# Cosformer attention into a two-layer FFN on one core: the third batch's x by DMA transposes, the first batch's result stored later, the order made anew

## The chip, the cores and the metric

The kernel runs on one core of a Trainium2 chip. The time is what the device takes for one execution, in microseconds (us); several runs are taken and their median is given. The engines are named as in the profile: PE is the matrix engine (TensorE), PEld its weight loads, DVE the VectorE, ACT the ScalarE, POOL the GpSimd, and SP the engine whose queue issues nearly all DMAs.

## The reference

Eight batches of attention with eight heads, 576 tokens and 64 features per head, with a linear (cosine) kernel, and then an FFN over all 4608 tokens:

```
phi(x) = concat(relu(x) * cos(theta), relu(x) * sin(theta))        # 64 -> 128 features
kv  = einsum('bhsf,bhsd->bhfd', phi(k), v);  z = sum over s of phi(k)
x   = (phi(q) @ kv) / (phi(q) . z + 1e-6)                          # 4608 x 512
h   = x @ w_in;  g = max(0.01 * h, h);  out = g @ w_out            # 512 -> 2048 -> 512
```

All inputs and the output are float32. The kernel rounds to float16 for the matmuls.

## The kernel before

Of each batch the first 512 tokens are the main part: 128 partitions by j = 0 to 3. The last 64 tokens of all eight batches together make a ninth group, number 8. So the FFN runs over nine groups g of 512 tokens. Batches are counted from 0 in the code and in this text: "batch 2" is the third.

For one batch the work is a chain. load_main and load_kvtail bring q, k and v (1 MB each, k and v with two tails of 64 KB) over the SP queue into a pool of three staging tiles. q_part and k_part apply phi on DVE or ACT (as the table ON says), v_part rounds v into the one tile vmain and its tails into vtail. kv_all forms kv and z on PE and copies them out on ACT. q_transpose_dma turns phi(q) of one j by a DMA transpose (qp to qpT). num multiplies it with kv on PE and divides on DVE (the small addition before it, den, on DVE or ACT), which gives xs, one j of x. x must then be turned (xT: features on partitions). For batches 3 and later x_transpose_dma does it with a DMA transpose on the SP queue; for batch 2 x_transpose does it with four PE transposes for each j into PSUM and one ACT copy out. Batches 0 and 1 have code of their own ahead of all this.

From group 2 on both layers of the FFN are computed with seven products of half-size blocks in place of eight, in Strassen's manner. In the first layer x_sums makes the sums of x's blocks on DVE, p1 is one product (four matmuls of 256 columns) into one of four PSUM banks, and seed, lrelu, u_copy, u_add and u_lrelu move it out. Product 1 (n = 1) needs only the xT of j = 0 and 1; the sums need all four. In the second layer g_sums makes the sums of g, p2 is four matmuls of one product, two banks a and b hold the results, and o_copy (ACT) and o_add (DVE) bring them into output tiles "ob" of two j each. Product 6 is added onto product 1 in bank a, after o_copy has read product 1 from there. o_store sends half of a group's 512 rows (512 KB). Group 1's first layer (f1_pair) is plain and runs while batch 2 goes through its attention; its second layer is in the seven products. Group 0's second layer is plain too: ffn2_out copies each of its four results into a tile "osb" and stores it at once, 256 KB each.

The order from batch 2 on is a table, PLACE: each step is put on a list with a number, the list is sorted by it, and the engines' instructions are issued in that order. What counts is the order on each engine: every engine and the SP queue works through its own instructions one after the other, and one that waits holds up those behind it. A DMA on SP also waits until the one eight before it has landed. A pool's tile is taken again only when its last readers are done, DMAs among them.

The first layer's and the second's matmuls are all on PE, and the two layers of neighbouring groups are interleaved in it, so that one fills the waits of the other.

Of the kernel before, what the change touches and what calls it, by code (L numbers as in the profile page):

```python
# [9 lines left out]
dt = mybir.dt  # L10
# [3 lines left out]
P = 128  # L14
# [4 lines left out]
def kernel(  # L19
# [14 lines left out]
    nc = tc.nc  # L34
# [35 lines left out]

    early = pool("early", 4, stack=first)
    pairpool = pool("pair", 2, stack=first)
    gpool = pool("g", 1, stack=first)
    opool = pool("osb", 4, stack=first)
# [410 lines left out]
    def x_transpose(g, j):  # L485
        xs = st["xs", g, j]
        ps = psum("o", [P, NKC, P], dt.float16, "ps_xt")
        for c in range(NKC):
            nc.tensor.transpose(ps[:, c, :], xs[:, 2 * c : 2 * c + 2, :], ident)
        nc.scalar.copy(xT_tile(g, j), ps)  # L490

# [63 lines left out]
    def ffn2_out(g, tt, eng):  # L555
        osb = opool.tile([P, DM], dt.float32, name="osb", tag="osb")
        copy(eng, osb, st["ps_o", g, tt])
        nc.sync.dma_start(out_rows(g)[:, tt, :], osb)
# [219 lines left out]
    opool = pool("out", 3)  # L778
# [287 lines left out]
    def open_seed():  # L1066
# [11 lines left out]
            16, 101, 252, 406, 552, 699, 827, 945,  # L1078
        ),
        "f1_pair": (  # L1080
            56, 57, 23, 24, 17, 18, 39, 42, 27, 28, 34, 35, 50, 51, 63, 70,
        ),
        "open_banks": (
            76,
        ),
        "open_seed": (
            77,
        ),
# [13 lines left out]
        ),  # L1102
        "seed": (
            100, 122, 168, 240, 259, 283, 309, 384, 408, 457, 483, 529, 569, 581, 612, 672, 712,
            734, 773, 822, 836, 868, 893, 935, 947, 988, 1003,
        ),
        "lrelu": (
# [4 lines left out]
        ),  # L1112
        "u_copy": (
# [4 lines left out]
        ),  # L1118
        "u_add": (
# [4 lines left out]
        ),  # L1124
        "u_lrelu": (
            186, 219, 248, 302, 326, 390, 402, 439, 486, 528, 543, 574, 610, 663, 697, 746, 775,
            805, 834, 869, 894, 932, 959, 977, 1018, 1038, 1041,
        ),
        "f1_one": (
            102, 104, 139, 147, 154, 155, 222, 224,  # L1130
        ),
        "o_tiles": (
            96, 228, 399, 546, 709, 854, 963, 1058,
        ),
# [204 lines left out]
```

## Time and profile before

| | us |
|---|---|
| median of three runs | 272.4 |
| lowest and highest | 272.4, 273.26 |
| the profiled execution's own time | 273.75 |
| its span, from the first to the last instruction | 271.9 |

Mean clock of PE in the profiled execution: 0.998. Busy shares of the span: PE 97%, PEld 82%, DVE 77%, ACT 72%, POOL 3%; the transfers of the SP queue fill 83.3% of 16 DMA engines' span. 57.05 MB were moved.

Rows of a timeline give the start and the length in us, then engine, line, operation and tiles. A row of groups gives a line, engine, operation, tiles and shapes, the count, busy us and mean ns of one, and the idle time of the engine just before them with what ended it. A row of stretches gives the stretch and its length, then busy us and count for PE, PEld, DVE, ACT and POOL, the granted clock of PE, the DMA share and GB/s. A matmul's busy time includes the way through the array, so neighbouring ones overlap.

### The profile page before, as it was taken

What the parts mean: (1) busy time and instruction counts of PE and PEld (TensorE: products, weight loads), DVE (VectorE), ACT (ScalarE), POOL (GpSimd) and SP (SyncE); (2) the same over time, 40 slices, a digit from 0 to 9 for tenths busy, and PEclk for the clock granted to TensorE, in tenths of its full rate; (3) what the DMA queues carried; (4) which work ended last, traced back from release to release, by engine and by line L of the source; (5) the groups of instructions that cost most, each with busy time, mean ns of one, the idle gap of its engine ahead of it and who ended that gap; (6) DMA issues with size and microseconds to landing.
All of it is one profiled execution on the core that took longest, in us unless ns stands there. A gap on an engine that the chain in (4) does not pass through costs nothing.

```text
span 271.9 us, 6680 instructions
## 1 busy us (share of the span) xinstructions
PE 263.6 (97%) x2703; PEld 221.8 (82%) x2703; DVE 209.3 (77%) x439; ACT 196.9 (72%) x329; POOL 8.1 (3%) x20
## 2 busy tenths in 40 slices
PE   8899999999999999999999999999999999999994
PEld 3585465555788989999999999999999889999983
DVE  4884998997969988999789869995686666765741
ACT  7675544786977887898687987887888766775621
POOL 2131011000000000000000000000000000000000
PEclk9999999999999999999999999999999999999999
DMA  6999999999999999999999999497178321300126
GB/s 216 382 384 403 381 410 356 292 221 239 222 306 226 238 199 226 301 174 246 224 266 209 244 284 269 80 194 176 39 82 195 112 55 68 157 0 2 77 80 154
DMA packets 82942, 57.05 MB, mean 210 GB/s; under 512 B 54496, under 2 KB 76000, under 8 KB 82400
## 3 DMA queue, kind: packets, MB, share of 16 engines
q1 hardware_dynamic: 82608, 56.37, 83.3%
q8 instruction: 21, 0.34, 0.6%
q10 hardware_dynamic: 304, 0.26, 0.4%
q14 instruction: 9, 0.07, 0.1%
HBM read 36.70 MB, written 9.44 MB: 170 GB/s over the span
## 4 chain that ended last, share of the span: by engine, by line
PE 72%; DMA 18%; ACT 3%; SPq 3%; DVE 1%; issue 1%; POOL 0%; ACTq 0%
PE ps_o L972 31%; PE ps_h L879 30%; DMA w2st<-in_moe_w_out_dram 6%; DMA w1st<-in_moe_w_in_dram 4%; PE ps_h L972 3%; DMA kpr<-in_k_dram 3%; DMA vst<-in_v_dram 3%; PE ps_num L417 2%; DMA qst<-in_q_dram 2%; SPq L130 2%; PE ps_kv L316 2%; ACT g L852 2%; PE ps_h L830 2%; PE ps_o L542 1%; ACT kp L254 1%
## 5 line engine op out<-in xcount | busy, mean ns | idle before, releaser
L972 PEld LDWEIGHTS <-g 128*128 128x128 f16 x640 | 62.2, 98 | 6.7
L267 DVE TENSOR_TENSOR u<-ps_h,u 128x512 f32<-128x512 f32 x54 | 37.1, 687 | 19.7 <-PE ps_h L879 17.9
L879 PEld LDWEIGHTS <-w 128*128 128x128 f16 x432 | 46.8, 114 | 1.4 <-issue 0.2
L972 PE MATMUL ps_o<-w,g 128*128 128x256 f16 x352 | 46.9, 273 | 0.0
L899 ACT COPY u<-ps_h 128x512 f32<-128x512 f32 x54 | 31.6, 586 | 9.8 <-PE ps_h L879 9.5
L892 ACT ACTIVATE g<-ps_h 128x512 f16<-128x512 f32 x54 | 31.9, 599 | 7.2 <-PE ps_h L879 6.4
L879 PEld LDWEIGHTS <-wa 128*128 128x128 f16 x324 | 33.5, 106 | 2.4
L879 PE MATMUL ps_h<-xw,w 128*128 128x256 f16 x216 | 32.1, 273 | 0.0
L879 PE MATMUL ps_h<-xT,w 128*128 128x256 f16 x216 | 31.8, 273 | 0.0
L972 PE MATMUL ps_o<-wb,g 128*128 128x256 f16 x232 | 31.5, 273 | 0.0
L879 PE MATMUL ps_h<-xw,wa 128*128 128x256 f16 x216 | 31.4, 273 | 0.0
L906 ACT ACTIVATE g<-u 128x1024 f16<-128x1024 f32 x27 | 28.7, 1062 | 2.9 <-DVE u L267 2.8
L990 ACT COPY ob<-ps_o 128x512 f32<-128x512 f32 (+1 forms) x32 | 18.0, 562 | 14.0 <-PE ps_o L972 11.9
L972 PEld LDWEIGHTS <-gs 128*128 128x128 f16 x256 | 24.6, 98 | 2.4
L435 DVE TENSOR_TENSOR xs<-ps_num,rden 128x512 f16<-128x512 f32 x28 | 19.3, 691 | 1.3
L830 PE MATMUL ps_h<-xT,w 128*128 128x512 f16 x80 | 19.2, 379 | 1.0 <-ACT g L852 1.0
L889 ACT COPY ps_h<-ps_h 128x512 f32<-128x512 f32 x27 | 15.7, 581 | 3.9 <-PE ps_h L879 3.5
L267 DVE TENSOR_TENSOR ob<-ps_o,ob 128x512 f32<-128x512 f32 (+1 forms) x22 | 14.8, 674 | 3.0 <-PE ps_o L972 2.0
L972 PE MATMUL ps_o<-wb,gs 128*128 128x256 f16 x120 | 17.0, 273 | 0.0
L972 PE MATMUL ps_o<-w,gs 128*128 128x256 f16 x120 | 16.5, 273 | 0.0
L879 PE MATMUL ps_h<-xT,wa 128*128 128x256 f16 x108 | 16.2, 273 | 0.0
L542 PE MATMUL ps_o<-w,g 128*128 128x512 f16 x64 | 15.6, 379 | 0.2 <-DVE w L264 0.2
(116 smaller groups left out, 392.1 us busy)
## 6 DMA issues: line engine op xcount, KB each, us to landing
qst<-in_q_dram SPq DMA_DIRECT2D x7, 1024.0 KB, 8.1
out_dram<-ob SPq DMA_DIRECT2D x14, 512.0 KB, 3.6
kst<-in_k_dram SPq DMA_DIRECT2D x6, 1024.0 KB, 7.2
vst<-in_v_dram SPq DMA_DIRECT2D x6, 1024.0 KB, 7.7
w1st<-in_moe_w_in_dram SPq DMA_DIRECT2D x8, 512.0 KB, 11.1
w2st<-in_moe_w_out_dram SPq DMA_DIRECT2D x4, 1024.0 KB, 13.1
vpr<-in_v_dram SPq DMA_DIRECT2D x4, 576.0 KB, 11.0
kpr<-in_k_dram SPq DMA_DIRECT2D x3, 576.0 KB, 11.1
```

What stands on the lines that cost most here:

```text
L130: nc.sync.dma_start(st[nm, b][:, lo:hi].rearrange("p c j d -> p c (j d)"), flat[:, lo:hi])
L267: nc.vector.tensor_tensor(out=o, in0=a, in1=b, op=ALU.add)
L435: nc.vector.tensor_tensor(out=xs, in0=ps[:, :, 0 : 4 * NE].rearrange("p a (b e) -> p a b e", e=NE)[:, :, :, 0:D], in1=rden.rearrange("p (a ...
L542: nc.tensor.matmul(ps, lhsT=st["g", g][:, m, tt * P : (tt + 1) * P], rhs=w2[:, m, :], start=(m == 0), stop=(m == NFT - 1),)
L830: nc.tensor.matmul(ps, lhsT=w1[m // 4][c // 2][:, c % 2, m % 4 : 512 : 4], rhs=st["xT", g][:, c], start=(c == 0), stop=(c == NKC - 1),)
L879: nc.tensor.matmul(bank[:, p], lhsT=w(c), rhs=x_blocks(g)[n][:, c], start=(fresh and p == 0 and c == 0), stop=(c == 1), skip_group_check=True,
L889: nc.scalar.copy(bank1[bj], bank1[bi])
L892: nc.scalar.activation(st["g" + nm, g][:, 2 * t : 2 * t + 2], bank1[bi], AF.Lrelu)
L899: nc.scalar.copy(st["u", g, t][:, n], bank1[bi])
L906: nc.scalar.activation(st["gt", g][:, :, 1, 2 * t : 2 * t + 2], st["u", g, t], AF.Lrelu)
L972: nc.tensor.matmul(bank, lhsT=st[G2[n], g][:, m, pair * P : (pair + 1) * P], rhs=W2[n](m), start=(fresh and m == 0), stop=(m == NH - 1), s ...
L990: nc.scalar.copy(o_at(g, half_, col, pair), bank_of(bi, pair, pair is None))
```

## The change

Three things are done. Batch 2's x is turned by DMA transposes like that of the later batches; x_transpose is gone. The output tiles' pool "out" (three) is split: two of its tiles ("out") are there from the start, one ("out1") opens later as before. Group 0's results go into the two early ones instead of four "osb" tiles, and are stored as two halves of 512 KB by o_store, at places of the table. And the table PLACE, with ON, is another one throughout.

```
-    opool = pool("osb", 4, stack=first)
+    outpool = pool("out", 2)
...
-    def x_transpose(g, j):
-        xs = st["xs", g, j]
-        ps = psum("o", [P, NKC, P], dt.float16, "ps_xt")
-        for c in range(NKC):
-            nc.tensor.transpose(ps[:, c, :], xs[:, 2 * c : 2 * c + 2, :], ident)
-        nc.scalar.copy(xT_tile(g, j), ps)
...
     def ffn2_out(g, tt, eng):
-        osb = opool.tile([P, DM], dt.float32, name="osb", tag="osb")
-        copy(eng, osb, st["ps_o", g, tt])
-        nc.sync.dma_start(out_rows(g)[:, tt, :], osb)
+        half_, pair = divmod(tt, 2)
+        if ("ob", g, half_) not in st:
+            st["ob", g, half_] = outpool.tile([P, 2, DM], dt.float32, name="ob", tag="ob")
+        copy(eng, st["ob", g, half_][:, pair], st["ps_o", g, tt])
...
-    opool = pool("out", 3)
+    opool = pool("out1", 1)
...
     def o_tiles(g):
-        for half_ in range(2):
-            st["ob", g, half_] = opool.tile([P, 2, DM], dt.float32, name="ob", tag="ob")
+        st["ob", g, 0], st["ob", g, 1] = (
+            pool_.tile([P, 2, DM], dt.float32, name="ob", tag="ob") for pool_ in (outpool, opool)
+        )
...
         "o_store": (
-            264, 347, 437, 500, 575, 615, 747, 956, 819, 872, 996, 1014, 1073, 1078,
+            225, 333, 390, 512, 568, 930, 763, 689, 870, 830, 986, 958, 1067, 1080, 192, 76,
         ),
...
+    for half_ in range(2):
+        put(o_store, 0, half_)
...
-            put((x_transpose_dma, x_transpose)[b == 2], b, j)
+            put(x_transpose_dma, b, j)
```

On the SP queue, from batch 2's v load (the first row) on, before. qpT<-qp are transposes of phi(q), first of batch 2, then of batch 3; qst, kst, vst and the tails ktl, vtl are the loads, from the third row on of batch 3.

```order
L103 DMA vst<-in_v_dram 128x8x256
L113 DMA vtl<-in_v_dram 64x4x64 x2
L558 DMA out_dram<-osb 128x512 x4
L385 DMA_TRANSPOSE qpT<-qp 128x8x128 x2
L103 DMA qst<-in_q_dram 128x8x256
L385 DMA_TRANSPOSE qpT<-qp 128x8x128 x2
L103 DMA kst<-in_k_dram 128x8x256
L113 DMA ktl<-in_k_dram 64x4x64 x2
L385 DMA_TRANSPOSE qpT<-qp 128x8x128
L103 DMA vst<-in_v_dram 128x8x256
L113 DMA vtl<-in_v_dram 64x4x64 x2
```

And the same stretch of the SP queue in the changed kernel, up to batch 4's q. xT<-xs are the transposes of batch 2's x, in the order j = 3, 0, 1, 2; out_dram<-ob is the second half of group 0's result.

```order
L104 DMA vst<-in_v_dram 128x8x256
L114 DMA vtl<-in_v_dram 64x4x64 x2
L386 DMA_TRANSPOSE qpT<-qp 128x8x128 x2
L104 DMA qst<-in_q_dram 128x8x256
L386 DMA_TRANSPOSE qpT<-qp 128x8x128
L104 DMA kst<-in_k_dram 128x8x256
L114 DMA ktl<-in_k_dram 64x4x64 x2
L386 DMA_TRANSPOSE qpT<-qp 128x8x128
L104 DMA vst<-in_v_dram 128x8x256
L114 DMA vtl<-in_v_dram 64x4x64 x2
L397 DMA_TRANSPOSE xT<-xs 128x4x128
L992 DMA out_dram<-ob 128x1024
```

The four stores of group 0 have left the place ahead of the transposes, one transpose fewer stands between the loads of q and v, and the transposes of x and a store stand behind v.

On ACT, before, from the copies of batch 2's turned x to the first cast of batch 3's v (vmain<-vst): ob<-ps_o is o_copy of group 1's first product, ps_h<-ps_h a seed, g and u the moving out of group 2's first products, qp and kp phi of batch 3.

```order
L490 COPY xT<-ps_xt 128x4x128
L254 ACTIVATE qp<-qst,cos_t 128x8x64
L254 ACTIVATE kp<-kst,cos_t 128x8x64 x2
L990 COPY ob<-ps_o_1235 128x2x256
L254 ACTIVATE kp<-kst,sin_t 128x8x64
L889 COPY ps_h_1233<-ps_h_1231 128x512
L254 ACTIVATE kp<-kst,cos_t 128x8x64
L863 ACTIVATE g<-ps_h_1232 128x2x256
L899 COPY u<-ps_h_1231 128x512
L262 CAST vmain<-vst 128x16x64
```

And on ACT in the changed kernel, from the last first-layer activations of group 1 (g<-ps_h) to the seed; den is a divide of batch 2.

```order
L846 ACTIVATE g<-ps_h 128x2x2x256
L255 ACTIVATE kp<-kst,cos_t 128x8x64
L846 ACTIVATE g<-ps_h 128x2x2x256
L431 ACTIVATE den<-ps_num,eps 128x8
L255 ACTIVATE kp<-kst,sin_t 128x8x64
L846 ACTIVATE g<-ps_h 128x2x2x256
L263 CAST vmain<-vst 128x16x64 x2
L985 COPY ob<-ps_o_1183 128x2x256
L255 ACTIVATE kp<-kst,sin_t 128x8x64
L883 COPY ps_h_1181<-ps_h_1179 128x512
```

The casts of v's main part, one on ACT before and two now, have moved from behind the first o_copy and the seed to ahead of both. The tile that this o_copy writes is the one from which the second half of group 0 is stored.

More of the change, by code (lines that the diff above doesn't have):

```diff
@@ L1077 @@
         "quarters": (
-            16, 101, 252, 406, 552, 699, 827, 945,
+            13, 112, 245, 400, 536, 699, 834, 951,
         ),
         "f1_pair": (
-            56, 57, 23, 24, 17, 18, 39, 42, 27, 28, 34, 35, 50, 51, 63, 70,
+            31, 32, 14, 18, 48, 54, 58, 60, 25, 26, 37, 39, 22, 23, 64, 67,
         ),
         "open_banks": (
-            76,
+            68,
         ),
         "open_seed": (
-            77,
+            72,
         ),
         "p1": (
[12 rows of a table removed]
[12 rows of a table added]
         ),
         "seed": (
-            100, 122, 168, 240, 259, 283, 309, 384, 408, 457, 483, 529, 569, 581, 612, 672, 712,
@@ L1128 @@
+            789, 829, 877, 913, 941, 962, 989, 1008, 1034, 1053,
         ),
         "f1_one": (
-            102, 104, 139, 147, 154, 155, 222, 224,
+            114, 116, 147, 150, 159, 160, 201, 202,
         ),
         "o_tiles": (
-            96, 228, 399, 546, 709, 854, 963, 1058,
+            84, 243, 405, 564, 718, 858, 970, 1060,
         ),
         "p2": (
[14 rows of a table removed]
[14 rows of a table added]
         ),
         "o_copy": (
-            97, 136, 174, 203, 229, 294, 330, 374, 400, 440, 480, 515, 547, 605, 638, 659, 710,
@@ L1153 @@
-            743, 770, 800, 855, 889, 906, 940, 964, 1009, 1025, 1045, 1064, 1071, 1086, 1097, 1059,
-            1085, 1095, 1100,
+            85, 115, 158, 203, 244, 275, 321, 359, 406, 458, 486, 532, 565, 598, 621, 658, 719,
+            745, 774, 803, 859, 881, 904, 932, 971, 1000, 1024, 1057, 1072, 1081, 1088, 1106, 1061,
+            1079, 1085, 1097,
         ),
         "o_add": (
-            146, 188, 213, 271, 348, 396, 428, 492, 558, 588, 642, 675, 740, 777, 804, 858, 918,
-            943, 976, 1032, 1068, 1091, 1087, 1110, 1082, 1101, 1107,
+            130, 194, 219, 282, 330, 380, 407, 493, 531, 582, 650, 674, 731, 793, 827, 862, 911,
@@ L1159 @@
+            957, 1006, 1035, 1062, 1091, 1098, 1112, 1092, 1094, 1108,
         ),
         "o_store": (
-            264, 347, 437, 500, 575, 615, 747, 956, 819, 872, 996, 1014, 1073, 1078,
+            225, 333, 390, 512, 568, 930, 763, 689, 870, 830, 986, 958, 1067, 1080, 192, 76,
         ),
         "o_store_tail": (
-            1092, 1104, 1108, 1111, 1109,
+            1093, 1100, 1107, 1113, 1110,
         ),
         "w1_sums": (
-            52, 178, 10, 13, 14, 325,
+            62, 109, 271, 294, 306, 299,
@@ L1203 @@
         ),
         "num": (
-            65, 49, 60, 53, 161, 190, 141, 131, 292, 280, 304, 337, 446, 429, 481, 461, 622, 576,
-            600, 590, 735, 772, 782, 757, 864, 888, 849, 873,
-        ),
-        "x_transpose": (
-            73, 61, 66, 62,
+            50, 70, 63, 55, 156, 182, 146, 172, 310, 326, 295, 342, 433, 467, 449, 489, 581, 630,
+            597, 606, 749, 725, 758, 776, 878, 890, 854, 836,
+        ),
+        "x_transpose_dma": (
+            82, 93, 94, 75, 163, 185, 177, 195, 318, 327, 354, 378, 478, 468, 511, 490, 620, 634,
+            639, 673, 775, 773, 797, 810, 910, 912, 897, 895,
@@ L1221 @@
         ),
         "load_qtail": (
-            676, 665, 702, 684,
+            777, 728, 769, 707,
         ),
@@ L1227 @@
         "k_part": (
-            "VVVAAAAVAVVVAAAVAVVVVVVVVVVAVVVAAAAVAVVAVAAVVVAVVVVAVVVVAAVA"
+            "VVVVVVAVAVVAAVVAAVVVVAAVAVVVVVAVVAAVVVAVVAAVAVVAVVAVVVAVVVVA"
         ),
         "q_part": (
-            "AVVAVVVAAVVVAVVAAAAAAVVVVAAAVVVAAVVVVVAVVVVAAAVAAAVAAAVA"
+            "AAAAAAVVVVAAVAVAAVVVVAVAAAVAVAAVVVVAVAVVVVVAAVVVAAVVVVVV"
         ),
         "v_part": (
-            "VVAAVVVAVVVVAVVAVV"
+            "VVAAAVAVVVVAVVVAAA"
         ),
         "num": (
-            "VVVVVVAVAVAVVVVVVVVVVVAVVVAV"
+            "AVAVVAAAAVVVVVVVAVVVVVVAVAVA"
         ),
```

28 lines of the change are left out of this document (12 added, 16 removed), and 102 rows, old and new, of the table PLACE.

## The prediction

> **What bounds the kernel now.** I read the page first.
>
> ```profile
> span 271.9 us, 6680 instructions
> PE 263.6 (97%) x2703; PEld 221.8 (82%) x2703; DVE 209.3 (77%) x439; ACT 196.9 (72%) x329; POOL 8.1 (3%) x20
> DMA  6999999999999999999999999497178321300126
> ```
>
> TensorE (PE) is busy for 97% of the span, and the DMA engines are full for the first two thirds. To see where the two meet I cut the span into stretches around the place that the change touches: before batch 2's x is used, the twelve microseconds after, and the rest.
>
> ```profile
> 50.90:73.28 22.38, 21.31 (x183) 13.56 (x182) 20.61 (x47) 18.02 (x27) 0.00 (x0) 1.00 1.10 230
> 73.28:82.00 8.72, 8.20 (x99) 7.21 (x97) 6.22 (x17) 6.85 (x12) 0.00 (x0) 1.00 1.14 310
> 82.00:262.00 180.00, 180.00 (x1890) 166.83 (x1889) 139.80 (x286) 139.89 (x237) 0.00 (x0) 1.00 0.78 166
> ```
>
> The first two columns are the length and PE's busy time; the last two are the DMA share and GB/s. From 82 us to 262 us PE never waits, so nothing there can be gained but work taken off PE. In the first stretch it waits 22.38 - 21.31 = 1.07 us, in the second 8.72 - 8.20 = 0.52 us, and there the DMA share is above 1: the transfers are saturated. The chain of waits for that region, and the issues on the SP queue (timeline), say which transfers:
>
> ```profile
> 57.86 6.57 DMA qst<-in_q_dram
> 65.87 1.82 ACT g L852 x2
> 67.69 1.54 ACT xT L490 x3
> 69.63 7.39 DMA vst<-in_v_dram
> 77.05 0.69 DVE vmain L264
> ...
> 50.72 3.18 SPq L558 DMA_DIRECT2D out_dram<-osb  x4
> 54.08 3.68 SPq L385 DMA_TRANSPOSE qpT<-qp  x2
> 59.52 4.76 SPq L385 DMA_TRANSPOSE qpT<-qp  x2
> 64.33 0.57 SPq L103 DMA_DIRECT2D kst<-in_k_dram  x1
> 66.46 3.12 SPq L385 DMA_TRANSPOSE qpT<-qp  x1
> ```
>
> Batch 3's q lands at 57.86 + 6.57 = 64.43, its v at 69.63 + 7.39 = 77.02. Between these two landings, in 12.6 us, the queue served two transposes of q, k with its tails, one more transpose and v. So around 50 to 80 us the end is set by what the DMA queue can deliver, and after 82 us by PE alone.
>
> **The change, part by part.** (1) TensorE loses 16 transposes, ScalarE (ACT) four copies out of PSUM.
>
> ```profile
> L489 PE MATMUL ps_xt<-ident,xs 128*128 128x128 f16 x16 | 1.4, 219 | 0.1
> L490 ACT COPY xT<-ps_xt 128x512 f16<-128x512 f16 x4 | 2.2, 589 | 0.0
> 48.44 0.45 PE ps_xth L474 x8
> ```
>
> The 219 ns are each one's own time; in a row they start 0.45 / 8 = 56 ns apart (eight like ones of batch 0), so PE is relieved of 16 x 56 ns = 0.9 us. The Trainium skill, "TensorE: Matmul & The Clock Gate", Part 4 on the PE-mode transpose, gives about 275 ns for one in a kernel; priced so, the change would save 4.4 us instead, and my time would come out 3.5 us lower. The trace's spacing decides against that price. The four copies, 2.2 us, stood in the chain at 67.69; they go with the waits below.
>
> (2) The four 256 KB stores of the first batch leave the SP queue at 50.72, and two of 512 KB take their place later: the first stands right behind batch 3's v load, the second some 20 us further on, where I see no reader waiting behind it. SP gets to the transposes of q 54.08 - 50.72 = 3.4 us sooner. The stores were 1.05 MB, at 295 GB/s (the mean of 40 to 60 us, next row) 3.5 us of transfer. So I take q to land 3.4 us sooner, at 61.0; had part of the stores' time been idle time of the queue, 2 us sooner, at 62.4.
>
> ```profile
> 40.00:60.00 20.00, 19.37 (x192) 11.27 (x190) 18.73 (x39) 13.82 (x22) 1.00 (x1) 1.00 1.06 295
> 57.85:59.80 1.95, 1.95 (x25) 1.22 (x23) 1.95 (x5) 1.74 (x3) 0.00 (x0) 1.00 1.10 217
> 71.12:77.03 5.91, 5.91 (x53) 5.24 (x51) 4.94 (x12) 5.02 (x9) 0.00 (x0) 1.00 1.21 235
> ```
>
> (3) The order of the SP queue. Between the landings of q and v there now stands one transpose less (256 KB, at the 217 GB/s of its stretch 1.2 us; I take 1.0): v lands at 61.0 + 12.6 - 1.0 = 72.6. Bounds: 71.3 if the loads of 1.2 MB each run at the 260 GB/s and better that single stretches show, 74.0 with the late q. Behind v now stand, in this order, its tails (128 KB), a transpose of x (128 KB), the store of half of batch 0's result (512 KB) and two more transposes of x (256 KB). At 250 GB/s, between the rows above, the store lands 3.1 us after v, at 75.7, and the x tiles of tokens 0 to 255 1.0 us after it, at 76.7; bounds for the store 2.6 us (the 310 GB/s of the second stretch) and 3.5 us (217).
>
> (4) The order on ACT. Before, the copy of batch 1's first output tile (o_copy) came ahead of any cast of batch 3's v. Now both casts of v's main part stand ahead of it, and it writes into the tile from which batch 0's half is stored, so it waits for that store also.
>
> ```profile
> L262 ACT CAST vmain<-vst 128x1024 f16<-128x1024 f32 x4 | 4.2, 1049 | 0.7 <-DMA vst<-in_v_dram 0.7
> L990 ACT COPY ob<-ps_o 128x512 f32<-128x512 f32 x28 | 16.5, 589 | 8.9 <-PE ps_o L972 8.8
> L972 PE MATMUL ps_o<-w,g 128*128 128x256 f16 x352 | 46.9, 273 | 0.0
> 94.16 2.62 PE ps_o L972 x24
> ```
>
> ACT sits at the first cast until v lands: 72.6 + 2 x 1.05 = 74.7; the store holds it to 75.7; o_copy ends at 75.7 + 0.59 = 76.3. Queued behind it on ACT are a seed copy and the activations that free PSUM. Waiting for it on PE are the eight matmuls that add P6 onto that bank (2.62 / 24 = 109 ns apart, 0.87 us), and behind those, in PE's order, the first product of batch 2's FFN (p1). So p1 starts at 76.3 + 0.9 = 77.2; the x tiles, at 76.7, would hold it nearly as long by themselves.
>
> (5) What p1's start says of the end.
>
> ```profile
> 73.28 0.60 PE L879 MATMUL ps_h<-xT,w 128*128 128x256 f16 x4
> 69.78 3.66 PE L972 MATMUL ps_o<-w,g 128*128 128x256 f16 x32
> ```
>
> p1 starts at 73.28 now, after 32 matmuls of batch 1's second layer; in the changed order 40 of them stand ahead of it, 0.87 us more, and 0.9 us of transposes less. The work ahead is thus equal: without any wait p1 would come about 1.1 us earlier than now, at 72.2. Behind p1 there are 271.9 - 73.28 = 198.6 us, less the 0.87 us moved ahead, less the 0.52 us of waits of the second stretch (its v now lands long before batch 3's kv needs it): 197.2 us. The end is 77.2 + 197.2 = 274.4 against 271.9, 2.5 us later. The remaining rows of the new order I cost at nothing: PE has 5 us more slack there against the same transfers, since it comes later to every load; if that cover is gone, the price is the second rival.
>
> The profiled execution took 273.75 us, 1.85 us more than its span; the median of the runs shown is 272.4, 0.5 us above the span. I add the difference to the median: 272.4 + 2.5 = **274.9 us**. With the early bounds (v at 71.3, store at 73.9) p1 starts at 75.4 and the time is 273.1; with the late ones (74.0 and 77.5, and the x tiles just behind) p1 starts at 79.0 to 79.5, which gives 277.2.
>
> **The rivals.** *The queue delivers in time.* The casts and the store keep pace with PE, and the change brings what it takes off: 0.9 us of transposes and the 1.07 + 0.52 us of waits, 269.9 us. It decides from p1's start: 271.9 - 197.2 = 74.7 is break-even, so the store has to land before 73.2, 2.5 us before my estimate. For it: v's load in the first trace was issued only at 69.63, behind a transpose that took SP 3.12 us, and the new order has it in the queue much sooner. Against it: a DMA share of 1.10 and 1.14 on both sides. Chance 0.15; that it ends half-way, within 0.3% of the old time (about what a measurement of this kernel can tell from no change), 0.13.
>
> *The transfers stay behind.* Batch 3's x needs four transposes behind k and v of batch 4, and PE, having waited once, waits again near 100 us. For it: the share stays above 1.1 until 160 us.
>
> ```profile
> 100.00:120.00 20.00, 20.00 (x233) 19.07 (x231) 18.12 (x39) 16.88 (x31) 0.00 (x0) 1.00 1.18 253
> ```
>
> Against it: PE's delay lets the queue gain on it. A second wait of about 2 us gives 276.9. Chance 0.10.
>
> *The clock falls.* If PE's wait is one piece, it is 77.2 - 72.2 = 5 us. At its start the trace shows a slow PE:
>
> ```profile
> 1.19 6.07 PE L189 MATMUL ps_idle<-blank 128*128 128x512 f16 x19 [1.19 <-DVE blank L182]
> 9.50 1.89 PE L189 MATMUL ps_idle<-blank 128*128 128x512 f16 x8
> 13.08 0.75 PE L348 MATMUL ps_kvh<-vpair,kp 64*128 64x65 f16 x36 [1.24 <-POOL vpair L264]
> ```
>
> Eight later ones take 1.89 us, 0.236 us each; at that pace the first 19 would have taken 4.5 us and not 6.07, so a cold start costs 1.6 us: 274.9 + 1.6 = 276.5 us. A gap of 1.24 us at 13 us did not bring it back, and I expect the wait in two pieces of 2 to 3 us, since the last num of batch 2 also waits (the divide ahead of it starts on ACT behind a feature map of batch 3's k, which lands late). Chance 0.07. The Trainium skill, same page, Part 1 on the clock gate, puts the limit at an idle window of about 3.4 us; by that rule two short waits are free and one of 5 us is not. No row here shows a gap long enough.
>
> **How the numbers follow.** My case has 0.55. Faster has 0.15, the same 0.13, slower 0.55 + 0.10 + 0.07 = 0.72. The range reaches down into the half-way case, to 271.3, leaving most of the first rival out, and up to 277.4, where late bounds and second waits end; what is beyond is a little over my late bound.
>
> **What would show it.** Right: in the profile after, PE idle before the P6 matmuls of batch 1 released by ACT's o_copy, with ACT waiting for v's load just ahead of it; batch 2's first p1 near 77 us; no PE idle from 85 us on. Wrong: p1 before 74.7 with no wait for o_copy or the x tiles (faster), or PE waits near 100 us and later (the second rival), or matmuls twice as far apart after the wait (the third).

## The result, and the profile after

| | before | after |
|---|---|---|
| median, us | 272.4 (9 runs, 272.38 to 273.26) | 275.56 (9 runs, 273.14 to 276.65) |
| ratio to before | | 1.0091, 95% interval 1.0068 to 1.0115 |
| profiled execution, us | 273.75, span 271.9 | 275.56, span 273.8 |

The change costs 0.9 per cent by the ratio; the medians lie further apart, 3.2 us, since the changed kernel's timings fall into two groups (see the run filled). The profiled execution of before was slower than all nine of its timings: executions of 272.4 us have a span of 270.6 us in the record of the later runs, not 271.9. The page of the changed kernel, PE's busy time and the granted clock in 40 slices:

```profile
PE 264.7 (97%) x2687; PEld 221.8 (81%) x2687; DVE 209.5 (77%) x435; ACT 194.2 (71%) x329; POOL 8.7 (3%) x20
PEclk9999999999979999999999999999999999999999
```

PE has 16 instructions less, and is yet busy longer. The twelfth slice of the clock, 75 to 82 us, is a 7 where the kernel before has a 9. The same three stretches as in the prediction (length, busy time by engine, then granted clock, DMA share, GB/s):

```profile
50.90:73.28 22.38, 20.35 (x167) 12.58 (x165) 20.35 (x45) 17.76 (x26) 0.00 (x0) 1.00 1.14 257
73.28:82.00 8.72, 7.53 (x75) 6.04 (x75) 5.64 (x13) 5.24 (x10) 0.00 (x0) 0.80 1.09 240
82.00:262.00 180.00, 180.00 (x1897) 167.11 (x1895) 140.03 (x286) 137.84 (x238) 0.00 (x0) 1.00 0.74 169
```

After 82 us PE again never waits, so all that is lost is lost before it. In the first stretch PE now waits 2.03 us, in the second 1.19, and in the second its clock stood at 0.80. The waits of PE that are not of the start-up, from the list of its waits (total, times, longest):

```profile
PE ps_o L966 <- ACT ob L985: 2.3, 1, 2.3
PE ps_num L418 <- DVE xs L436: 1.0, 2, 0.7
```

The timeline around the larger one, ACT's rows first, then PE's:

```profile
70.06 1.99 ACT L263 CAST vmain<-vst 128x1024 f16<-128x1024 f32 x2 [1.14 <-DMA vst<-in_v_dram]
73.83 0.59 ACT L985 COPY ob<-ps_o 128x512 f32<-128x512 f32 x1 [1.78 <-DMA out_dram<-ob]
74.47 1.03 PE L966 MATMUL ps_o<-wb,gs 128*128 128x256 f16 x8 [2.26 <-ACT ob L985]
75.34 0.96 PE L873 MATMUL ps_h<-xT,w 128*128 128x256 f16 x4
76.09 1.91 PE L966 MATMUL ps_o<-wb,gs 128*128 128x256 f16 x8
79.62 1.04 PE L873 MATMUL ps_h<-xw,wa 128*128 128x256 f16 x8
```

ACT waits for v, casts it, then waits 1.78 us for the store that holds the tile of its next copy (o_copy); PE stands 2.26 us behind that copy, and p1 begins at 75.34. Then comes what looked unlikely: eight matmuls take 1.91 us at 76.09, and eight of the same size 1.04 at 79.62. The clock was down to half from 75.43 to 78.85 us, after the wait had ended:

```profile
72.02:75.43 3.41, 1.15 (x11) 0.89 (x10) 3.38 (x9) 1.24 (x3) 0.00 (x0) 1.00 1.05 257
75.43:78.84 3.41, 3.41 (x18) 2.46 (x17) 3.38 (x8) 1.82 (x3) 0.00 (x0) 0.50 1.02 289
```

The store on the chain of waits, and the SP queue around it (issues; the start and the length of each):

```profile
67.58 6.18 DMA out_dram<-ob
```

```profile
64.00 0.53 SPq L104 DMA_DIRECT2D vst<-in_v_dram  x1
67.58 0.57 SPq L992 DMA_DIRECT2D out_dram<-ob  x1
```

### The profile page after: what moved, and what is told of

The parts are those of the page before. It is cut to its first block, busy times and chain, and to the rows that moved or that the text cites. A ratio compares the mean times of both kernels' runs of the same rounds, so it can differ in the third digit from the quotient of the medians.

```text
span 273.8 us, 6625 instructions
## 1 busy us (share of the span) xinstructions
PE 264.7 (97%) x2687; PEld 221.8 (81%) x2687; DVE 209.5 (77%) x435; ACT 194.2 (71%) x329; POOL 8.7 (3%) x20
## 4 chain that ended last, share of the span: by engine, by line
PE 92%; DMA 4%; DVE 2%; ACT 1%; issue 0%; SPq 0%; DVEq 0%; ACTq 0%
PE ps_o L966 32%; PE ps_h L873 31%; PE ps_o L534 5%; PE ps_h L824 4%; PE ps_idle L190 4%; PE ps_h L497 4%; PE ps_h L966 3%; PE ps_num L418 2%; DMA out_dram<-ob 2%; PE ps_kv L317 2%; DMA ktl<-in_k_dram 2%; PE ps_hq L516 1%; PE ps_qt L405 1%; PE ps_xth L475 1%; DVE kp L282 1%; PE ps_numh L453 1%
## 5 line engine op out<-in xcount | busy, mean ns | idle before, releaser
L966 PE MATMUL ps_o<-w,g 128*128 128x256 f16 x352 | 45.8, 273 | 0.0
L873 PE MATMUL ps_h<-xT,w 128*128 128x256 f16 x216 | 32.6, 278 | 0.0
L966 PE MATMUL ps_o<-wb,g 128*128 128x256 f16 x232 | 30.9, 273 | 0.0
L966 PE MATMUL ps_o<-w,gs 128*128 128x256 f16 x120 | 15.9, 272 | 0.0
```

The costliest lines, as they stand in the source:

```text
L873: nc.tensor.matmul(bank[:, p], lhsT=w(c), rhs=x_blocks(g)[n][:, c], start=(fresh and p == 0 and c == 0), stop=(c == 1), skip_group_check=True,
L966: nc.tensor.matmul(bank, lhsT=st[G2[n], g][:, m, pair * P : (pair + 1) * P], rhs=W2[n](m), start=(fresh and m == 0), stop=(m == NH - 1), s ...
```

## The experiments

Each was timed in five rounds beside the kernel before. In the diffs, the numbers of the table PLACE are places in the program's order.

| run | edit | median, us | ratio to before, 95% interval |
|---|---|---|---|
| casts_behind | v's casts behind o_copy | 275.54 | 1.0114 (1.0093 to 1.0134) |
| free_tile | o_copy into a tile that no store holds | 273.54 | 1.0048 (1.0028 to 1.0068) |
| both | the two | 273.99 | 1.0078 (1.0048 to 1.0108) |
| all_three | and the store behind x on the queue | 272.78 | 1.0006 (0.9992 to 1.0021) |
| filled | PE kept busy in the wait | 274.09 | 1.0058 (1.0035 to 1.0081) |
| store_early | stores where they were before | 275.84 | 1.0118 (1.0093 to 1.0143) |
| transposes_alone | kernel before, x by DMA | 277.44 | 1.0188 (1.0151 to 1.0225) |
| stores_alone | kernel before, stores late | 273.05 | 1.0021 (1.0005 to 1.0038) |
| nums_first | all_three, q's and k's feature maps later | 272.73 | 1.0003 (0.9981 to 1.0024) |
| swapped | nums_first, tiles that p1 needs first | 272.25 | 0.9983 (0.9967 to 0.9999) |
| pe_left | nums_first, two of four x tiles by PE | 272.40 | 0.9995 (0.9979 to 1.0011) |
| x_first | swapped, x ahead of v on the queue | 274.77 | 1.0078 (1.0049 to 1.0107) |

### The two things that hold o_copy

**casts_behind**

```
 "v_part": ( 20, 28, 29,
-    83, 77, 96,
+    85.4, 85.2, 96,        # o_copy stands at 85
```

> The changed kernel with one edit: on ScalarE the two casts of batch 3's v stand behind the copy of batch 1's first output tile (o_copy), not ahead of it. Theory (two things hold o_copy, and the later one is the store: in the changed kernel's trace the casts end at 72.05 us, the store lands at 73.76 and o_copy starts at 73.83): o_copy starts at about 73.8 as before, its wait grows from 1.78 to some 3 us, PE waits the same 2.3 us, and the time stays at 275.6 us, within 0.5. The casts now start at 74.4 and push the seed copy back to 76.5, which can cost up to 0.5 us more. Rival (v's landing is what holds PE): o_copy starts near 71, PE does not wait there, and the time falls by 2 us or more, to 273.5 or below.

```profile
75.49 1.86 PE L966 MATMUL ps_o<-wb,gs 128*128 128x256 f16 x8 [2.85 <-ACT ob L985]
```

As expected: with the casts away the wait is still there, 2.85 us, and it ends by the store alone. Of the two waits that the prediction put one behind the other, the later one decides. This trace too shows the half-speed stretch (eight matmuls in 1.86 us), and the mean clock is 0.991 or 0.992 in four of the six timings.

**free_tile**

```
-            pool_.tile(...) for pool_ in (outpool, opool)
+            pool_.tile(...) for pool_ in (
+                (outpool, opool) if g > 2 else (outpool, outpool) if g > 1 else (opool, outpool)
+            )
```

> The changed kernel with one edit: batch 1's first output half goes into a tile that no store holds (the two halves of batch 1 change tiles), the store and the casts stay where they are. Theory: o_copy follows the casts at 72.05, its matmuls on PE wait some 0.5 us instead of 2.26; batch 2's first product (p1) then waits for the DMA-transposed x of tokens 128 to 255, which landed at 74.64, about 1 us. p1 starts at 74.7 instead of 75.34 (0.65 us sooner), and since no wait is longer than about 1.2 us the slow stretch after it is gone (8 matmuls of p1 took 1.91 us where they take 1.04 later: some 1.9 us over the stretch): 275.6 - 0.65 - 1.9 = 273.0 us. Rival A (the slow stretch has nothing to do with the wait): 274.9. Rival B (x itself is what is late, and the wait for it takes the place of the whole 2.26 us): 275.6, p1 at 75.3.

PE's rows of this run, and two links of its chain of waits:

```profile
73.29 1.03 PE L966 MATMUL ps_o<-wb,gs 128*128 128x256 f16 x8 [0.53 <-ACT ob L987]
75.63 0.60 PE L873 MATMUL ps_h<-xT,w 128*128 128x256 f16 x4 [1.31 <-DMA xT<-xs]
76.07 1.04 PE L966 MATMUL ps_o<-wb,gs 128*128 128x256 f16 x8
```

```profile
69.96 0.69 DVE xs L436
70.68 4.82 DMA xT<-xs
```

The wait of 2.26 us became two, of 0.53 and 1.31 us, the second for x itself. p1 did not come sooner (75.63), as rival B has it, though not at its time of 275.6 us: the matmuls behind it run at full pace, the mean clock is 0.997 or more in all seven timings, and the ratio is 1.0048, against 1.0091 (the intervals just touch). Since p1 is not sooner, what the free tile saved is the clock. And the store had hidden another bound: x of the last tile is divided at 70.65 and lands by its DMA transpose at 75.50.

**both**

```
 # v_part as in casts_behind, tiles as in free_tile
```

> Both edits: the casts of v behind o_copy, and a free tile for it. Theory: o_copy starts as soon as PE has made its tile, near 70.6 us, and nothing on PE waits for it; p1 still waits for the transposed x (74.64), in one piece of some 1.5 us: p1 at 74.7, so the same time as with the free tile alone, 273.0 us. If a single wait of 1.5 us is enough to slow the clock, 274.5. Rival (x is there in time once ScalarE is freed, because its landing is moved by what runs ahead of it): p1 near 72.9, 271.0 us.

```profile
75.40 0.60 PE L873 MATMUL ps_h<-xT,w 128*128 128x256 f16 x4 [1.85 <-DMA xT<-xs]
```

No wait at o_copy, and p1 still at 75.40: with ScalarE out of the way x alone holds it, 1.85 us in one piece. The theory's 74.7 was 0.7 us too early, as x lands later here. The interval (1.0048 to 1.0108) overlaps that of the free tile, so no gain by the casts can be seen. The clock stayed up in the profiled execution, but two of the six timings have a mean clock of 0.994 (275.22 and 276.38 us); how long PE waited in those is not on record.

**all_three**

```
 "o_store": ( ... 1067, 1080, 192,
-    76,
+    103.5,                 # behind the x transposes
```

> Both edits and a third: the store of batch 0's first half is moved on the SP queue from ahead of three of batch 2's x transposes to behind them (ahead of batch 4's q load). Theory: without 512 KB in front of them the x tiles of tokens 0 to 255 land about 2 us sooner, at 72.6, p1 starts at 72.9 instead of 75.34 and nothing slows down: 275.6 - 2.4 - 1.9 = 271.2 us, which would be 0.4 per cent below the kernel before. Rival (the queue is saturated and what is moved back comes due later, at batch 4's q and k or batch 3's q): the time falls only to 272.5 to 273, with new PE waits between 80 and 110 us.

PE's waits in its timeline:

```profile
64.10 0.42 PE L418 MATMUL ps_num<-kv,qpT 128*128 128x65 f16 x8 [1.28 <-DVE xs L436]
69.18 0.42 PE L418 MATMUL ps_num<-kv,qpT 128*128 128x65 f16 x8 [0.52 <-DVE xs L436]
74.74 0.60 PE L873 MATMUL ps_h<-xT,w 128*128 128x256 f16 x4 [1.00 <-DMA xT<-xs]
```

With 512 KB less ahead of x, p1 comes at 74.74 and the loss is gone: 1.0006. The 271.2 us expected were not reached, since p1 was to start at 72.9. The time is the rival's (272.5 to 273), but its waits did not come: no wait of PE follows up to 200 us. Three are left ahead of it, 2.8 us in all.

### Is the slow stretch made by the wait?

**filled**

```
+    def warm_fill(n):
+        for _ in range(n):
+            nc.tensor.matmul(
+                bank1[0].rearrange("p h n -> p (h n)"), lhsT=none, rhs=w2[:, 0, :]
+            )
...
+    line.append((91.5, warm_fill, (8,)))
```

> The changed kernel with nothing moved, and eight extra matmuls of zeros (128x512, some 0.24 us each, 1.9 us together) on PE just ahead of the matmuls that wait for o_copy; they write a bank that p1 overwrites, so they add work that the output doesn't need and lie inside the wait of 2.26 us. Theory (the wait itself slows the clock): o_copy, the wait's end (74.5) and p1's start (75.3) stay, the granted clock stays at 1.00 after it in every run, and p1's matmuls run at 109 ns each: the slow stretch of some 1.9 us is gone, 275.6 - 1.9 = 273.7 us, about what the free tile gave. Rival (the clock falls for another reason, or the loss was the landing of data alone): no change, 275.6 us.

```profile
72.14 1.89 PE L1070 MATMUL ps_h<-w,none 128*128 128x512 f16 x8
74.80 1.03 PE L966 MATMUL ps_o<-wb,gs 128*128 128x256 f16 x8 [0.78 <-ACT ob L985]
75.67 0.60 PE L873 MATMUL ps_h<-xT,w 128*128 128x256 f16 x4
76.11 1.04 PE L966 MATMUL ps_o<-wb,gs 128*128 128x256 f16 x8
```

p1 starts 0.3 us later than in the changed kernel, but at full pace, and the mean clock is 0.997 or more in all six timings. By the time alone the useless work isn't shown to pay (1.0058 against 1.0091, the intervals overlap); the clock is what tells. In the nine timings of the changed kernel the mean clock is 0.991 to 0.993 in five (275.56 to 276.65 us, mean 275.96) and 0.997 to 0.999 in four (273.14 to 274.35, mean 273.93). If a timing's clock fell by chance five times in nine, six in a row without a fall would have a chance of under 1 per cent, (4/9)^6. So the wait does slow the clock. The slow stretch costs 2.0 us where it comes, and the landing of data alone, the rest of the loss, some 1.5 us (273.93 - 272.4).

### The parts of the change by themselves

**transposes_alone** (on the kernel before)

```
-        ps = psum("o", [P, NKC, P], dt.float16, "ps_xt")
-        for c in range(NKC):
-            nc.tensor.transpose(ps[:, c, :], xs[:, 2 * c : 2 * c + 2, :], ident)
-        nc.scalar.copy(xT_tile(g, j), ps)
+        nc.sync.dma_start_transpose(
+            out=xT_tile(g, j), in_=xs.rearrange("p h d -> p (h d)")
+        )
```

> The kernel before with one part of the change alone: batch 2's x is turned by four DMA transposes on the SP queue at the places where PE turned it, all else in the old order. Theory: PE loses 0.9 us of work; the four transposes of 128 KB stand in the SP queue ahead of batch 3's v (about 0.5 us each at 240 GB/s), so v lands some 2 us later than 77.0, at 79, and the kv of batch 3, which waited 0.35 us for its cast at 78.14, waits some 2 us more: 272.4 - 0.9 + 2.1 = 273.6 us. p1 at 73.3 or a little sooner, since the x tiles land at 70 to 72. Rival A (the transposes themselves hold p1: they land 4 to 6 us after their issue, as in the changed kernel): p1 at 75 to 76 and 275 us. Rival B (the queue has room): 271.5 us.

The chain of waits, then PE's timeline:

```profile
73.28 1.21 SPq L487
74.59 2.43 DMA xT<-xs
```

```profile
77.16 1.02 PE L878 MATMUL ps_h<-xT,w 128*128 128x256 f16 x4 [4.50 <-DMA xT<-xs]
77.97 1.91 PE L829 MATMUL ps_h<-xT,w 128*128 128x512 f16 x4
```

Rival A, and worse than it said: SP issues the four transposes one after the other up to 74.59, the last lands at 77.02, PE stands 4.5 us and then runs at half speed (four matmuls of 512 columns in 1.91 us). In all six timings the mean clock is 0.994 or less. Alone, the part that names the change costs 1.9 per cent.

**store_early** (on the changed kernel)

```
 "o_store": ( ... 1067, 1080,
-    192, 76,
+    0.2, 0.1,
```

> The changed kernel with one edit: both stores of batch 0's result stand on the SP queue where the four stores stood in the kernel before (ahead of batch 2's q transposes), not behind batch 3's v and later. Theory (step 2 of the prediction: 1 MB of stores in front delays all that follows by 3.4 us): batch 3's q lands at 64.5 instead of 61.2, k at 68.5, v at 72 to 73.4; nothing holds o_copy's tile, but the casts end at 74 to 75.5, o_copy at 75 to 76, p1 at 76 to 77, and the num of batch 2 that waits for q's landing costs PE up to 3 us already near 65: 277 to 278.5 us. Rival (the queue has idle time there, early stores cost nothing): v at 70, o_copy at 72.6, p1 near 73.5 to 74.7: 272.5 to 273.5 us.

ACT's waits for q and v, then PE's waits:

```profile
63.70 0.72 ACT L255 ACTIVATE qp<-qst,sin_t 128x512 f16<-128x512 f32 x1 [2.43 <-DMA qst<-in_q_dram]
73.75 1.99 ACT L263 CAST vmain<-vst 128x1024 f16<-128x1024 f32 x2 [2.67 <-DMA vst<-in_v_dram]
```

```profile
65.83 0.41 PE L418 MATMUL ps_num<-kv,qpT 128*128 128x65 f16 x8 [3.21 <-DVE xs L436]
76.28 1.03 PE L966 MATMUL ps_o<-wb,gs 128*128 128x256 f16 x8 [1.79 <-ACT ob L985]
77.15 0.60 PE L873 MATMUL ps_h<-xT,w 128*128 128x256 f16 x4
```

q lands at 63.6 and v at 73.7, 2.4 and 3.7 us later than with the late stores, and PE pays near 65 us, about as expected. p1 comes at 77.15, just behind the 76 to 77 expected, and yet the total, 275.84, is below the 277 to 278.5: the expectation put the end too far behind p1 (196.8 us follow it in this trace). Where the store stands makes no difference to the sum that these runs can tell (1.0118 against 1.0091, overlapping intervals): early it delays q, late it holds o_copy. In the profiled execution the clock stayed up; four of the other timings have a mean clock of 0.988 to 0.994.

**stores_alone** (on the kernel before; the tiles of batch 1's and later results follow a fixed rotation of three)

```
-        nc.sync.dma_start(out_rows(g)[:, tt, :], osb)
...
+    for half_ in range(2):
+        line.append(((140.5, 111.5)[half_], o_store, (0, half_)))
```

> The kernel before with another part of the change alone: batch 0's result stays in two tiles of 512 KB, and its two stores stand on the SP queue behind batch 4's q load and behind batch 3's x, not ahead of batch 2's q transposes; PE turns batch 2's x and the order is otherwise the old one. Theory (step 2 of the prediction): batch 3's q lands 3 us sooner, at 61.0 to 61.8 instead of 64.4, v at 73.5 to 74.5 instead of 77.0; the waits of PE ahead of p1 (0.54 us at 66.83) and for kv (0.35 at 78.14) go: 272.6 - 1.1 = 271.5 us, p1 at 72.2 to 72.8. With the run of the transposes alone this would say that the change is one part that costs some 4.8 us, one that brings 1, and an order that makes up for the rest. Rival (PE's order holds nothing that an earlier landing lets through, because q and k are waited for in other places): 272.6, same as before. Rival B (batch 1's second output tile waits for the late store): 273.5 or more, with a wait of ScalarE at a copy into ob near 80 to 90 us.

The stretches (82 to 100 us by itself), and the wait in the last one:

```profile
50.90:73.28 22.38, 22.24 (x192) 14.34 (x191) 21.73 (x51) 19.39 (x30) 0.00 (x0) 1.00 1.00 231
73.28:82.00 8.72, 8.72 (x113) 8.01 (x111) 7.04 (x18) 7.71 (x15) 0.00 (x0) 1.00 1.24 299
82.00:100.00 18.00, 16.62 (x154) 14.23 (x153) 14.61 (x33) 12.79 (x23) 0.00 (x0) 1.00 1.09 226
```

```profile
96.88 1.04 ACT L263 CAST vmain<-vst 128x1024 f16<-128x1024 f32 x1 [1.91 <-DMA vst<-in_v_dram]
98.47 0.60 PE L881 MATMUL ps_h<-xT,w 128*128 128x256 f16 x4 [1.00 <-ACT g L865]
```

The waits up to 82 us are gone, all but 0.14 of 1.59 us, as step 2 said, and p1 starts at 71.75. But 1.38 us come back between 82 and 100 us, 1.00 of them when ACT sits at batch 4's v and PE behind it, which fits a queue that has the megabyte still to carry. So no expectation holds in full: the time is near that of the first rival, some 0.2 per cent above before.

### What is left, and whether it can be had back

**nums_first**

```
 # all_three, and
-    k_part ... 57, 59, 61, 65     q_part ... 44, 47
+    k_part ... 70.1 to 70.4       q_part ... 50.1, 50.2
```

> The three edits of the run before (casts behind o_copy, free tile, store behind x) and two more of the same kind: on ScalarE and VectorE two feature maps of batch 3's q and four of its k, which wait for landings at 61.9 and 66.1 us, stand behind batch 2's num divides instead of ahead of them. In the trace with the three edits PE still waits 1.28 us near 63.7 (num of batch 2 for the divide ahead of it, held on ScalarE by q's feature map), 0.52 near 69 (the same with k's) and 1.00 at p1 (x of tokens 128 to 255, which follows that last num). Theory: all three go, 272.8 - 2.8 = 270.0 us, or 270.5 if x still lands 0.5 us late; p1 near 72. Rival (what is moved back comes due as waits of PE between 75 and 110 us, or the queue, being saturated, lands x as late as before): 271.8 to 272.8 us.

```profile
64.29 0.41 PE L418 MATMUL ps_num<-kv,qpT 128*128 128x65 f16 x8 [0.62 <-DVE xs L436]
74.18 0.60 PE L873 MATMUL ps_h<-xT,w 128*128 128x256 f16 x4 [0.79 <-DMA xT<-xs]
```

Two of the three waits shrink from 1.80 to 0.62 us together, and p1 still waits for x: 74.18. The time is as with the three edits. The rival's second half holds: x lands nearly as late, whatever PE did before.

**swapped**

```
 # nums_first, and for batch 2
-    x_transpose_dma  82, 93, 94, 75       q_transpose_dma  12, 43, 7, 30
+    x_transpose_dma  75, 76, 93, 82       q_transpose_dma  12, 7, 43, 30
 # q_part and num of tiles 1 and 2 exchanged likewise
```

> The five edits of the last run (nums first) and the roles of token tiles 1 and 2 of batch 2 exchanged: tile 1's q is cast, transposed and turned into x where tile 2's was, and the queue issues the x transposes in the order 0, 1, 3, 2 instead of 3, 0, 1, 2. p1 needs tiles 0 and 1 alone. Theory: what is left of the loss is the time from the last num that p1 needs (xs ended at 70.4) to the landing of its DMA transpose (74.05), while PE has work for only 2.7 us of it; with tile 1 ready at some 66.5 the transposes of tiles 0 and 1 stand directly behind v's tails and land near 72.3, p1 starts at 72.5 instead of 74.18: 272.7 - 1.5 = 271.2 us (0.5 per cent below the kernel before), less if the third and fourth x tile, at some 74.7, hold the whole-row matmuls (f1_one) that follow. Rival (x's landing is set by v's megabyte ahead of it in the queue, whatever the order): p1 at 73.5 or later and 272 to 272.7.

```profile
73.81 0.60 PE L873 MATMUL ps_h<-xT,w 128*128 128x256 f16 x4 [1.87 <-DMA xT<-xs]
```

The rival's landing: x is issued at 66.1 instead of 70.4 and is there only 0.4 us sooner, because v's megabyte lies ahead of it in the queue. Still 272.25 us, 0.9983 of before: of the twelve runs it is the only one whose interval lies below 1, and that by 0.0001, which chance alone could give.

**pe_left**

```
 # nums_first, and for batch 2
-            put(x_transpose_dma, b, j)
+            put((x_transpose_dma, turn_pe)[b == 2 and j < 2], b, j)
 # turn_pe: the four transposes and the copy of the kernel before, places 67.5 and 85.1
```

> The five edits of the run nums first, and token tiles 0 and 1 of batch 2's x turned by PE and copied by ScalarE as in the kernel before; tiles 2 and 3 stay with the DMA transposes. Theory: the path from xs to a usable x is 0.2 us of PE and 0.6 of ScalarE instead of 3.6 to 5.7 us of queue, so x of tile 1 is there at 71.5 and p1 starts when PE is free, at 72.2 plus the 0.45 us of the eight transposes: 272.7 - 74.18 + 72.7 = 271.2 us; the full rows wait at most a little for tiles 2 and 3 (74.7). Rival (PE is bound by other landings then, batch 3's v or k): 272 to 272.7 us with new waits behind p1.

```profile
72.05 1.99 ACT L263 CAST vmain<-vst 128x1024 f16<-128x1024 f32 x2 [1.20 <-DMA vst<-in_v_dram]
73.63 1.05 PE L973 MATMUL ps_o<-wb,gs 128*128 128x256 f16 x8 [0.79 <-DVE gs L271]
75.20 0.60 PE L880 MATMUL ps_h<-xT,w 128*128 128x256 f16 x4 [0.52 <-ACT ps_h L890]
```

x no longer holds p1, which starts at 72.24 without a wait; behind it PE waits 0.79 and 0.52 us for sums on VectorE and a seed on ScalarE, both of which stand behind casts of v, and ACT had waited for v's landing. PE also does 0.45 us more work. The rival: 272.4 us.

**x_first**

```
 # the casts of v here behind the seed and the g sums; from swapped:
-    loads ... 73
+    loads ... 76.5                # v, behind two x transposes
```

> The run swapped, with batch 3's v load moved on the SP queue from ahead of batch 2's x transposes of tiles 0 and 1 to behind them, and, since v then lands later, its casts moved behind the seed copy on ScalarE and its tail's behind the g sums on VectorE. In the trace of swapped PE has one wait left there: 1.87 us at p1, for x tiles issued at 66.1 and 67.5 behind v's 1 MB and landed at 73.16 and 73.67. Theory (a transpose on this queue costs what stands ahead of it): both x tiles land at 68 to 70.5, long before PE gets to p1 at 71.9, so the 1.87 us go; v lands at 72 to 72.5 and its casts end at 75, about when batch 3's kv comes: 272.25 - 1.5 to 1.9 = 270.4 to 270.8 us, 0.7 per cent below the kernel before. Rival (v is as urgent as x: its casts hold what PE needs next, the lrelu and copies that free PSUM, or kv): the wait moves behind p1, some 1.5 us near 75 to 77, and the time stays at 272.2.

```profile
75.33 1.99 ACT L263 CAST vmain<-vst 128x1024 f16<-128x1024 f32 x2 [1.86 <-DMA vst<-in_v_dram]
72.21 0.60 PE L873 MATMUL ps_h<-xT,w 128*128 128x256 f16 x4
76.92 1.05 PE L824 MATMUL ps_h<-xT,w 128*128 128x512 f16 x4 [1.95 <-DMA xT<-xs]
```

p1 comes at 72.21 without a wait, as the theory had it, and behind it PE stands 1.95 us, up to 76.92, for the other two x tiles, now behind v. Moreover SP issued v only at 68.24, behind the two transposes, and not at 63.85 as in swapped, so v came at 75.3 and not at 72. The time is 2.5 us longer than with v ahead.

## Why the prediction was right, and where not

The sign was right, and so was the wait: PE stands behind o_copy, which waits for v, casts it, and then waits for the late store. That 274.9 lies so near 275.56 is luck, for the sum has three errors that nearly cancel. p1 came 1.9 us sooner than forecast and 0.4 us less follows it; the slow clock, which the sum left out, adds 1.7 us; and the base was 1.3 us too low (step 5): 274.9 - 1.9 - 0.4 + 1.7 + 1.3 = 275.6. Of the forecast's own signs, the wait at o_copy and the quiet after 85 us came; p1 near 77 did not; and the third rival's sign, matmuls twice as far apart, came too.

**Step 1, what PE sheds:** 16 instructions fewer, as said; no run prices them by themselves.

**Step 2, q sooner:** right. q was to land at 61.0, and VectorE gets it at 61.25:

```profile
61.25 0.49 DVE L257 TENSOR_SCALAR qp<-qst,sin_t 128x512 f16<-128x512 f32 x1 [0.34 <-DMA qst<-in_q_dram]
```

**Step 3, the SP queue:** the term that was mis-sized. v was there at 70.06, not 72.6, and outside the bounds (71.3 to 74.0); the store let go of its tile at 73.8, not 75.7. I carried over the 12.6 us that lay between the landings of q and v before. In that time SP had been held at a transpose that took it 3.12 us, and issued v only at 69.63, 5.2 us after q's landing; now it issues v at 64.00, 2.8 us after it. I read the interval of before as transfers; part of it was waiting of the issuer, of which the new order has less (the first rival had named it, and I gave it too little weight). The interval between the landings is now some 8.9 us. Of the 3.7 us that it lost, 2.4 lie ahead of v's issue, and the rest in v's own way, 6.0 us instead of 7.4.

**Step 4, the order on ACT:** right in kind, both waits are in the trace in the order given. That of the two the store decides is shown by casts_behind. o_copy ended at 74.4 instead of 76.3 and p1 started at 75.34 instead of 77.2, all of it from step 3. The remark that the x tiles "would hold it nearly as long by themselves" was the more important half, and the runs free_tile and both show it: without any wait for the store p1 starts at 75.6 and 75.4.

**Step 5, the end from p1:** the length behind p1 was nearly right, the base was not. 197.2 us were to follow p1; 273.8 - 75.34 = 198.5 did, of which the second stretch lost 8.72 x 0.20 = 1.7 us to the clock, so that 196.8 are left. In the seven later runs whose profiled clock stayed up and whose order behind p1 holds no further wait (free_tile, both, all_three, filled, store_early, nums_first, swapped) the span less p1's start is 196.7 to 196.9 us. The base: I set the new end against the span of the profiled execution, 271.9, and added the difference to the median, 272.4; but that execution took 273.75 us, and one of 272.4 us has a span of 270.6. So break-even for p1 was 270.6 - 196.8 = 73.8 and not 74.7, and swapped, with p1 at 73.81, is indeed level. Where the profiled execution of before lost its 1.3 us isn't shown, as no trace of a faster one is on record. (The stretch that the prediction calls twelve microseconds long is 8.7.)

**The rivals.** With p1 at 75.34 and break-even at 73.8 the landings alone cost 1.5 us, which is what the four timings at full clock show; the slow stretch, 3.41 us at half the clock, adds 1.7, and together that is the 3.2 us between the medians. So that the loss is 0.9 per cent and not some 0.5 is due to the third rival, the clock. It was given 0.07 because I expected two waits of 2 to 3 us to be harmless; one of 2.26 us was enough, in five of nine timings. Its price, 1.6 us, was well taken from the start-up (1.7 in the trace, 2.0 between the two groups of timings). The first rival, a queue that delivers in time, was closer than its chance of 0.15 said: p1 missed its stated break-even, 74.7, by 0.6 us, though the one that the medians give by 1.5. The second, waits near 100 us, did not come in the changed kernel; it came in stores_alone, with the old order.

The Trainium skill, "TensorE: Matmul & The Clock Gate", Part 1, on which the prediction leaned beside this rival, has the clock fall after an idle window of about 3.4 us, free-running. The traces agree with the grid of such windows: in the changed kernel the full clock was granted at 7.17 us, fell 68.27 us later, twenty times 3.41, and came back after 3.41. They do not agree that a whole window must be idle, and here the measurement decides: the clock fell behind a window of which 2.26 us were idle (the two rows in the section on the result), and in the profiled execution of store_early it did not fall after a wait of 3.21 us, which lay across two windows with 1.6 us in each. PE's busy time there, of 3.4 us, in the two windows, and in the window of x_first's long wait:

```profile
60.82:64.24 3.42, 1.80 (x16) 0.81 (x13) 0.55 (x2) 0.99 (x2) 0.00 (x0) 1.00 1.19 283
64.24:67.65 3.41, 1.82 (x16) 1.14 (x17) 2.80 (x7) 2.57 (x5) 0.00 (x0) 1.00 1.13 322
75.03:78.44 3.41, 1.51 (x10) 1.11 (x11) 2.34 (x7) 3.11 (x4) 0.00 (x0) 1.00 0.89 217
```

**What the change comes to.** The transposes by DMA cost 1.9 per cent in the old order, the late stores alone 0.2; the transposes in the new order with the stores early (store_early) cost 1.2, and all of it 0.9. In the old order the transposes thus cost more than in the new one. Not all of the loss is theirs, though: three edits of the new order alone (all_three) take it away. The new order with x still turned by PE was not run, so what the order is worth by itself stays open. With no store or cast in the way the kernel is where it was before (1.0006 and 1.0003, and 0.9983 at best): in all_three PE waits 2.8 us ahead of p1, where the kernel before waits 1.6 up to 82 us, so the 0.9 us that PE sheds go into waits for data.

That what is left is the queue's delivery is what the runs point to: each order of v, x and the store on the queue moved the wait (num, o_copy, p1, the whole rows behind p1, batch 4's v) and none removed it. It isn't shown by taking load off the queue; whether a second queue for loads or stores would help wasn't tried.

## What to carry to other kernels

A transpose by DMA costs what stands ahead of it in its queue: here 2.4 to 7.0 us from the issue to a usable tile of batch 2 in the runs above, against some 0.8 us by PE and a copy (four times 56 ns and 0.59 us), so it pays only where the reader comes that much later. When an order is judged, look at what an in-order engine has queued behind each wait for a landing, and when a store must release a tile; removing the last of several waits shows the next. And an idle PE is not charged by the microsecond: a wait of 2.26 us cost nearly as much again in slow matmuls. Cutting it in two (free_tile) or filling it (filled) kept the clock up in every timing of those two runs.

## What the runs showed of the hardware

- The granted clock changes on a grid of 3.41 us that starts when it is first granted. It fell to 0.5 for 3.41 us in the traces of the changed kernel and casts_behind, and for 6.83 us in that of transposes_alone, and matmuls then started twice as far apart (eight of 256 columns in 1.91 instead of 1.04 us).
- What decides in these traces is PE's idle time within one window of the grid. In all 14 of them (before, after and the twelve runs) each whole window with 2.26 us or more of it was followed by half the clock (2.26, 2.43 and 3.07 us inside the kernel, the others at its end), and no window with 1.90 us or less made the clock fall. So the limit lies between, and a single wait may pass or not by where it falls in the grid.
- That fits the timings, of which only the mean clock is known. An estimate, with a limit of 2.0 us and waits placed at random in the grid: a wait of 2.26 us falls in about half of the executions, one of 2.85 in two thirds, one of 3.21 in three quarters. A mean clock under 0.995 was seen in five of nine (after), four of six (casts_behind) and four of six (store_early), and in all six with 4.5 us (transposes_alone). It was also seen in two of six of both, one of six of x_first and one of twelve of nums_first, whose profiled executions show no wait over 1.95 us; the executions with the lower clock were not traced.
- Eight matmuls with a tile of zeros in the wait, 1.89 us of them, kept the clock up in all six timings.
- A transpose of 128 KB on the SP queue landed 2.4 us after its issue at the least and 6.6 at the most (median 3.3 over all 28 of x in the changed kernel).
- No DMA of SP was issued before the one eight places ahead of it had landed, in 143 issues of the kernel before and 145 of the changed one.
